# Padding rows scattered by row numbers, and two weight subtractions on VectorE

## The chip, the core and the metric

One core of a Trainium2 chip runs the whole program. The metric is the device time in microseconds of one launch; what is given for a kernel is the median of its runs. Engines: PE (TensorE), VectorE (DVE), ScalarE (ACT), GpSimd (POOL), and SyncE (SP), which only issues DMAs.

## What is computed

A linear attention (random features, exponentials) gives 4608 token rows of 512 numbers. Each row then goes through one of 8 experts, the one whose embedding is most alike, and is weighted by the softmax of that choice:

```python
xn = x / (np.linalg.norm(x, axis=-1, keepdims=True) + 1e-06)
logits = xn @ en.T / tau
expert_idx = np.argmax(logits, axis=1)
...
for e in range(E):
    mask = expert_idx == e
    if not mask.any():
        continue
    h = np.maximum(x[mask] @ w1[e], 0.0)
    out[mask] = gate_w[mask, None] * (h @ w2[e])
```

N = 4608, D = 512, E = 8, F = 1024; w1 is 512 x 1024 and w2 1024 x 512 for each expert.

## The kernel before

**First part** (to about 212 us): the attention, tile by tile of 128 tokens. As soon as a tile's tokens have their experts, GpSimd scatters its rows (L592, an indirect DMA with one row number for each partition) into `xs`, a table in device memory with a region of `REG` rows for each expert. Beside the 512 numbers a row carries the logits and the token's number, `PAY` = 521 numbers in all. `run[e]` is the next free row of region e.

**Pads.** The second part reads `xs` in blocks of 128 rows, so the last block of an expert reaches past its tokens. Rows of padding (`padrow`, in a part of w1l that is not in use yet, with a token number that no store takes) are written there: 128 rows from `run[e]` on, for every expert. The first expert, the one with most tokens, is swapped to place 0 and padded by SyncE (`pad(0)`); behind a drain, `pad(1)` to `pad(7)` load a row number into a register of GpSimd and issue a plain DMA of 128 rows (L990 to L1000).

**Second part** (from about 223 us): 38 steps of 128 rows. Step t takes its rows by `xload` (L188), splits them into a high and a low half (h and l, products in three passes), multiplies by w1 (24 matmuls of 512 columns), by w2 (24 more), and stores to the output. Steps 0 and 1 are done in the first part, step 2 begins the second. Weights lie in two buffers of four quarters each. The first expert's stand in buffer 0; the quarters 0 to 3 of the next go to buffer 1 during steps 2 to 5: a load to `raww` (`wload`), a high half by ScalarE, a low half by subtraction (`wsplit`, L227). For quarters 0 to 3 w1's low half is VectorE's work and w2's GpSimd's (L233, L234). Step 4 waits for w1's quarter 3.

**Order.** PE, GpSimd and SyncE run in the order of the code, in the second part VectorE and ScalarE too; between the two parts VectorE's order is the scheduler's. SyncE's queue holds all loads, one behind the other. Waits come from a tracker of memory: who writes a tile waits for whoever still reads or writes the same place, also where a pool was closed and another one opened on its memory. The pool `once`, which holds the tables between the parts, closes with the first part; `p2`, with the buffers `xg3`, `xg4` of the steps' rows, opens behind it. For accesses to `xs` the waits are set by hand: `written` takes them away among writes, and `xload` names which earlier writes a load waits for. For step 3 (t == NPRE + 1) the last PADP - 1 writes, the pads on GpSimd, are left out, and step 4's load waits for all.

Of the kernel before, what the change touches and what calls it, by code (L numbers as in the profile page):

```python
# [13 lines left out]
I32 = mybir.dt.int32  # L14
# [3 lines left out]
ALU = mybir.AluOpType  # L18
AX = mybir.AxisListType
ET = mybir.EngineType  # L20
PSUM = bass.MemoryType.PSUM

P = 128
B, H, S, D, M = 8, 8, 576, 64, 128
E, F = 8, 1024
# [7 lines left out]
GPICK = 5  # L33
DUM = E * REG
ROWS = DUM + P
RS = 576
PAY = DM + E + 1
NQ = 4
LAG = 7
NPRE = 2  # L40
# [1 line left out]
LOADS = {29: 0, 30: 2, 31: 1, 33: 4, 35: 6, 36: 3, 37: 5, 39: 7}  # L42
LOADS_LATE = 33
FILLS = {36: 1, 37: 1, 38: 1, 39: 1, 40: 1, 41: 1, 42: 2, 43: 4, 44: 5}
PADP = 8
ONACT = 3
DRAINS = (4,)
KPROJ = {0: (0,), 1: (1, 2), 2: (3,), 3: (4,), 4: (5,), 5: (6,)}
# [14 lines left out]
WHY = "computed on the chip from counts that sum to the token number"  # L63
# [3 lines left out]
def attention_moe(ctx: ExitStack, tc: tile.TileContext, qT, kT, v1, omT, emb, tau, w1q, w2q, xs, out):  # L67
    nc = tc.nc
# [39 lines left out]
    stepf = const.tile([P, 1], F32, name="stepf")  # L108
# [15 lines left out]
    runi = const.tile([P, E], I32, name="runi")  # L124
# [10 lines left out]
    put, got, outs, last_x, junks, kept = [], [], [], [], [], {}  # L135
# [4 lines left out]
    padrow = w1l[:, 1, 2, 0:PAY].bitcast(F32)  # L140
# [41 lines left out]
    def written(w):  # L182

        for o in put + got:
            tc.declare_no_dep(w.ins, o.ins.name, reason="other rows")
        put.append(w)

    def xload(t, row, xg):  # L188
        r = nc.sync.dma_start(xg, xs[ds(row, P), 0:PAY])
        if t in range(NPRE + 3):  # L190
            for j, w in enumerate(put):
                if t < NPRE and j > 3 * GPICK + 3 and w is not kept.get(t) or t == NPRE + 1 and j > len(put) - PADP:

                    tc.declare_no_dep(r.ins, w.ins.name, reason="other rows")
                else:
                    tc.add_manual_dep(r.ins, w.ins.name, sync, reason="rows written in any order")
        else:
            tc.add_manual_dep(r.ins, last_x[0].ins.name, sync, reason="behind an earlier step's wait")
        got.append(r)
        last_x[:] = [r]  # L200
        return xg
# [6 lines left out]
    def apart(wn, ws, t, ms, o):  # L208

        if (t == o or (t < NQ and o < NQ)) and (o, t) not in ((0, 3), (1, 2), (2, 3)):
            for w in ws:
                for m in ms:
                    tc.declare_no_dep(max(w, m, key=seq.get).ins, min(w, m, key=seq.get).ins.name, reason="the other weight buffer")
# [11 lines left out]
    def wsplit(wn, t, raw, dv, dp):  # L227
        _, h, l = W[wn]
        at = lambda a, d: a.rearrange("p a q f -> p (a q) f")[:, ds(d, 1), :].rearrange("p o f -> p (o f)")
        if t is not None and t < NQ:  # L230

            ih = nc.scalar.activation(h[:, 1, t, :], raw, AF.Copy)  # L232
            eng = nc.vector if wn == "w1" else nc.gpsimd  # L233
            ils = [eng.tensor_tensor(l[:, 1, t, :], raw, h[:, 1, t, :].bitcast(F32), op=ALU.subtract)]  # L234
        else:
            ih = nc.vector.tensor_copy(at(h, dv), raw)  # L236
            ils = []
            piece = F if t is None or t >= NSTAT - 2 else PIECE
            eng, d = (nc.vector, dv) if wn == "w2" and t is not None and t >= NSTAT - 2 else (nc.gpsimd, dp)
            for c in range(0, F, piece):  # L240
                c = slice(c, c + piece)
                ils.append(eng.tensor_tensor(at(l, d)[:, c], raw[:, c], at(h, d)[:, c].bitcast(F32), op=ALU.subtract))  # L242
        if t is None:
            return
        for w in (ih, *ils):
            seq[w] = len(seq)
            if t >= NQ:
                tc.add_manual_dep(w.ins, mmi[wn, t - 1][-1].ins.name, sync, reason="the buffer's last use")
        for o in range(NSTAT):
            apart(wn, (ih, *ils), t, mmi.get((wn, o), ()), o)  # L250
        if t < NPRE:

            for w in put:
                for il in ils:
                    tc.declare_no_dep(il.ins, w.ins.name, reason="another part of the weights")
        for w in spl.get((wn, t - 1), ())[1:]:
            tc.declare_no_dep(ih.ins, w.ins.name, reason="another part of the weights")
        spl[wn, t] = (ih, *ils)
# [3 lines left out]
    def flush():  # L262
        while lows:
            lows.pop(0)()
# [60 lines left out]
    with ExitStack() as c1:  # L325
# [453 lines left out]
        for i in range(NTILE + LAG + 2):  # L779
# [15 lines left out]
            if i == XLOAD:  # L795
                prow = [nc.values_load(
                    firsti[0:1, t : t + 1], engines=[ET.SP], min_val=t * P, max_val=(E - 1) * REG + t * P,
                    skip_runtime_bounds_check_because=WHY) for t in range(NPRE + 1)]
                for t in range(NPRE):
                    xload(t, prow[t], xgp[t])  # L800
# [181 lines left out]
        vt = nc.vector  # L982
        t = lambda n, w=E, dt=F32: once.tile([P, w], dt, name=n)
# [3 lines left out]
        vt.tensor_copy(runi[:, 0:1], swp[:, 0:1])  # L987
        vt.tensor_scalar(swp[:, 1:2], run[:, 0:1], swp[:, 0:1], None, op0=ALU.subtract)
        vt.scalar_tensor_tensor(runi[:, 1:], isf[:, 1:], swp[:, 1:2], run[:, 1:], op0=ALU.mult, op1=ALU.add)
        def pad(e):  # L990
            eng, et = (nc.gpsimd, ET.Pool) if 0 < e < PADP else (nc.sync, ET.SP)
            v = nc.values_load(runi[0:1, e : e + 1], engines=[et], min_val=0, max_val=DUM - P, skip_runtime_bounds_check_because=WHY)  # L992
            written(eng.dma_start(xs[ds(v, P), 0:PAY], padrow))

        pad(0)
        xload(NPRE, prow[NPRE], xgp[NPRE])

        nc.gpsimd.drain()
        for e in range(1, PADP):
            pad(e)  # L1000


        row = lambda a: a.unsqueeze(1).to_broadcast([P, E, E])
# [58 lines left out]
        tp = pb[3]  # L1062
        nc.tensor.transpose(tp[0:5, 0:P], tab, ident)
        vt.tensor_copy(tabi, tp[0:5, 0:NSTEP])
        for _ in range(FILL3):
            next(fill, None)
            flush()
# [15 lines left out]
    def x_of(t, row):  # L1083
        return xload(t, row, xgp[0] if t == "x" else xgp[1] if t == SHIFT else ring[(t - NPRE - (t > SHIFT)) % len(ring)])
# [6 lines left out]
    def words(t):  # L1091
        return p2.tile([P, F + DM], F32, name=f"wd{t}", tag="wd", bufs=1)
# [35 lines left out]
    def split(wn, t):  # L1128
        if t < NSTAT:
            wsplit(wn, t, raws.pop((wn, t)), *((reg("dv", t), reg("dp", t)) if t >= NQ else (None, None)))  # L1130
# [19 lines left out]
    with tc.manual_schedule(engines={ET.PE, ET.Activation, ET.DVE, ET.Pool, ET.SP}):  # L1150
# [11 lines left out]
        def joined(u):  # L1162
            wd, n = words(u), turn[u][0].shape[1] * P
            assert n == F
            for k in range(2):
                rejoin(u, wd, 0, F, k)
            return wd, n
# [65 lines left out]
        for t in range(NPRE, NSTAT):  # L1233
# [11 lines left out]
            if early:  # L1245
                wn = joined(t - 1)
# [43 lines left out]
            if late and not early:  # L1290
                wn = words(t - 1), turn[t - 1][0].shape[1] * P
# [64 lines left out]
    with tc.If(tot > NSTAT):  # L1356
        with tc.For_i(NSTAT, tot, 1) as i:
            get = lambda k, eng, mx: nc.values_load(tabi[k : k + 1, ds(i, 1)], engines=[eng], min_val=0, max_val=mx, skip_runtime_bounds_check_because=WHY)
            xgl = x_of("x", get(0, ET.SP, DUM))
            src = get(2, ET.SP, E * NQ - 1)  # L1360
            rw = {wn: wload(wn, "x", src) for wn in W}
            par = get(1, ET.PE, 1)
            h = hidden("x", x_turned("x", xgl), par)
            po = bank("pox", "kv0")
            products(po, h_turned("x", h), "w2", par, range(8), 0, True, True)
            n2, total = few("n2", "x", 3)[:, 0:1], few("total", "x", 3)[:, 0:1]
            squares(xgl, n2, nu[0])
            nrm = root(gp, n2, 1, "x")
            norms(nrm)
            exps(xgl, nrm, total)  # L1370
            inverted(total)
            scaled(po, xgl, total)
            store("x", xgl)
            dv, dp = get(3, ET.DVE, 2 * NQ - 1), get(3, ET.Pool, 2 * NQ - 1)
            for wn in W:
                wsplit(wn, None, rw[wn], dv, dp)
# [49 lines left out]
```

## Time and profile before

| | us |
|---|---|
| median of 3 runs | 630.5 (629.82 to 630.67) |
| the profiled execution, its own time | 630.09 |
| its span, first to last instruction | 628.4 |

The rows further down come from that one execution; their times are us from the span's start. PE's busy time says little about how fast it runs; where a chain of waits goes through PE, the time between two starts tells its pace. A wait for several signals is put down to the one that came last. Landing times are counted from the start of the issue to the completion signal.

### The profile page before, as it was taken

Reading aid. Unit: us, or ns where it says so; the run is one execution under the profiler, and the core shown is the slowest. Engines: PE = TensorE matmul, PEld = TensorE weight load, DVE = VectorE, ACT = ScalarE, POOL = GpSimd, SP = SyncE. Lnnn points to the kernel's source line nnn. Section 1 sums busy time; section 2 is a strip of 40 time slices with the busy share of each in tenths; the row PEclk is TensorE's granted clock in tenths of the full one; section 3 lists DMA queues with packets and bytes.
Section 4 is the critical chain, followed back from the end, with each engine's and each line's share of the span. In section 5 each row is a group of like instructions: output and inputs, shape, how many; then the busy total and the mean of one; then the engine's idle time right before and its main releaser. Section 6 shows DMA issues by size and latency. Waiting matters only on the chain.

```text
span 628.4 us, 19172 instructions
## 1 busy us (share of the span) xinstructions
PE 620.4 (99%) x6337; PEld 531.1 (85%) x6338; DVE 496.5 (79%) x917; ACT 432.5 (69%) x1135; POOL 421.2 (67%) x603
## 2 busy tenths in 40 slices
PE   9999999999999999999999999999999999999996
PEld 8999999999988787888888888888888888888885
DVE  5799899898989836779787877887887886877764
ACT  6999899899888237675757566656666656575630
POOL 3013344456887534588898878896987989796862
PEclk9999999999999999999999999999999999999999
DMA  7754776777772487698787796867787775968731
GB/s 259 221 154 156 240 198 206 223 220 237 274 254 79 154 305 253 187 273 233 225 217 238 180 263 189 244 191 211 226 211 243 201 245 171 255 196 197 221 118 47
DMA packets 143263, 132.19 MB, mean 210 GB/s; under 512 B 107766, under 2 KB 107894, under 8 KB 143168
## 3 DMA queue, kind: packets, MB, share of 16 engines
q1 hardware_dynamic: 136544, 109.96, 60.7%
q0 software_dynamic: 6480, 20.91, 8.6%
q8 instruction: 57, 0.93, 0.6%
q14 instruction: 38, 0.31, 0.2%
q10 hardware_dynamic: 144, 0.07, 0.0%
HBM read 83.78 MB, written 21.97 MB: 168 GB/s over the span
## 4 chain that ended last, share of the span: by engine, by line
PE 89%; issue 3%; DVE 3%; POOL 1%; ACT 1%; DMA 1%; POOLq 1%; DVEq 0%; ACTq 0%
PE po L287 30%; PE pb L287 30%; PE pb L376 11%; PE kva L408 5%; PE nuu L485 5%; PE nuu L465 2%; PE fs_a L287 1%; PE nuu L408 1%; DMA raww<-w2q 1%; DVE nmq L380 1%; PE pb L94 1%; POOLq L992 0%; PE pb L435 0%; DMA qt<-qT 0%; POOL w2l L234 0%
## 5 line engine op out<-in xcount | busy, mean ns | idle before, releaser
L242 POOL TENSOR_TENSOR w2l<-raww,w2h 128x256 f32 x128 | 140.3, 1096 | 7.6
L242 POOL TENSOR_TENSOR w1l<-raww,w1h 128x256 f32 (+1 forms) x130 | 116.0, 892 | 14.5 <-DMA xgp<-xs 5.2
L287 PE MATMUL po<-w2h,hh 128*128 (+1 forms) x288 | 112.3, 390 | 0.0
L287 PE MATMUL po<-w2l,hh 128*128 (+1 forms) x288 | 112.1, 389 | 0.0
L287 PE MATMUL po<-w2h,hl 128*128 (+1 forms) x288 | 112.1, 389 | 0.0
L287 PE MATMUL pb<-w1h,xh 128*128 (+1 forms) x280 | 109.6, 391 | 0.3 <-ACT nuu L298 0.3
L287 PE MATMUL pb<-w1h,xl 128*128 (+1 forms) x280 | 109.2, 390 | 0.0
L287 PE MATMUL pb<-w1l,xh 128*128 (+1 forms) x280 | 109.0, 389 | 0.0
L1140 DVE COPY pl<-pb 128x512 uint16<-128x512 uint16 x68 | 46.8, 690 | 59.8 <-ACT pl L1136 59.1
L1136 ACT ACTIVATE pl<-pb 128x512 uint16<-128x512 uint16 x68 | 39.4, 582 | 67.9 <-PE pb L287 65.2
L390 ACT ACTIVATE ftq<-pb,nmq 128x128 f32<-128x128 f32 x288 | 80.1, 415 | 4.2 <-DVE nmq L380 4.2
L317 POOL DMA_INDIRECT y<-xgp,tail x36 | 44.6, 1239 | 54.0 <-DVE w1h L236 30.2
L390 ACT ACTIVATE ftk<-pb,nmk 128x128 f32<-128x128 f32 x272 | 75.9, 466 | 4.5 <-DVE nmk L380 4.5
L1158 DVE COPY wd<-t 128x1024 uint16<-128x1024 uint16 x68 | 65.1, 959 | 1.6 <-DMA t<-pl 1.5
L1174 ACT ACTIVATE hh<-wd 128x1024 fp32r<-128x1024 f32 x34 | 36.1, 1063 | 42.1 <-DVE wd L1158 37.1
L287 PEld LDWEIGHTS po<-w2h,hl 128*128 128x128 f32 x288 | 54.1, 188 | 11.4
L287 PEld LDWEIGHTS po<-w2h,hh 128*128 128x128 f32 x288 | 54.1, 188 | 11.1
L287 PEld LDWEIGHTS po<-w2l,hh 128*128 128x128 f32 x288 | 54.0, 187 | 11.1
L287 PEld LDWEIGHTS pb<-w1h,xh 128*128 128x128 f32 x280 | 52.5, 188 | 11.3 <-ACT w2h L232 0.7
L287 PEld LDWEIGHTS pb<-w1h,xl 128*128 128x128 f32 x280 | 52.5, 188 | 11.2 <-DVE xl L271 0.2
L287 PEld LDWEIGHTS pb<-w1l,xh 128*128 128x128 f32 x280 | 52.7, 188 | 10.8
L1178 DVE SCALAR_TENSOR_TENSOR hl<-wd,hh 128x1024 fp32r<-128x1024 f32 x34 | 54.7, 1610 | 2.9 <-ACT hh L1174 2.3
(351 smaller groups left out, 1250.0 us busy)
## 6 DMA issues: line engine op xcount, KB each, us to landing
raww<-w1q SPq DMA_DIRECT2D x38, 512.0 KB, 4.5
raww<-w2q SPq DMA_DIRECT2D x38, 512.0 KB, 4.8
qt<-qT SPq DMA_DIRECT2D x36, 256.0 KB, 3.1
kt<-kT SPq DMA_DIRECT2D x35, 256.0 KB, 3.6
xg<-xs SPq DMA_DIRECT2D x23, 260.5 KB, 2.8
xgp<-xs SPq DMA_DIRECT2D x15, 260.5 KB, 3.6
rf<-w1q SPq DMA_DIRECT2D x4, 512.0 KB
rf<-w2q SPq DMA_DIRECT2D x4, 512.0 KB, 3.9
```

What stands on the lines that cost most here:

```text
L242: ils.append(eng.tensor_tensor(at(l, d)[:, c], raw[:, c], at(h, d)[:, c].bitcast(F32), op=ALU.subtract))
L287: done.append(nc.tensor.matmul(dst, x[:, c * P : (c + 1) * P], ws.rearrange("p o f -> p (o f)"), start=(begin and i == 0 and k == 0), stop ...
L317: w = nc.gpsimd.indirect_dma_start(out=out, out_offset=bass.IndirectOffsetOnAxis(ap=(xg[:, DM:] if tail is None else tail)[:, E : E + 1].b ...
L376: nc.tensor.matmul(st["pj" + w, i, a][:, c, :], st[w, i][r, c, :], om[r, :], start=True, stop=True)
L390: nc.scalar.activation(ft[:, h, :], pj[:, h, :], AF.Exp, bias=nm[:, h : h + 1])
L408: nc.tensor.matmul(acc[c : c + 64, h, :], ft[:, h, c : c + 64], vt[:, 2 * h + a, :], start=begin and h == 0, stop=u == 4 + 4 * b and h == 3,)
L485: nc.tensor.matmul(pn[a][s * D : s * D + D, h, :], st["qp", i, s][:, 2 * h + a, :], kvs[sb, int(u > 4 - s)][:, 4 * a + h, :], start=True, ...
L1136: nc.scalar.activation(planes[1][:, o : o + 512], halved(src)[:, :, 1], AF.Copy)
L1140: nc.vector.tensor_copy(planes[0][:, o : o + 512], halved(src)[:, :, 0])
L1158: nc.vector.tensor_copy(to, src)
L1174: nc.scalar.activation(hh, wd[:, 0:F], AF.Relu)
L1178: nc.vector.scalar_tensor_tensor(hl, wd[:, 0:F], 0.0, hh.bitcast(F32), op0=ALU.max, op1=ALU.subtract)
```

## The change

Pads 1 to 7 no longer are plain DMAs of 128 rows from a register's row number. Four VectorE operations make a table `padi` of row numbers, 128 for each expert: `run[e]` plus the partition's number, and for partitions that would pass the next multiple of 128 a number above `ROWS`, which the DMA's bounds check leaves out. Seven indirect DMAs on GpSimd, behind the step table, take their row numbers from its columns. `padi` is a tile of the pool `once`. The constant `PADP` (8) gives way to `E` (8). And in `wsplit`, for w2's quarters 0 and 1, the subtraction goes from GpSimd to VectorE.

```diff
--- before.py
+++ after.py
@@ -42,7 +42,6 @@
 LOADS = {29: 0, 30: 2, 31: 1, 33: 4, 35: 6, 36: 3, 37: 5, 39: 7}
 LOADS_LATE = 33
 FILLS = {36: 1, 37: 1, 38: 1, 39: 1, 40: 1, 41: 1, 42: 2, 43: 4, 44: 5}
-PADP = 8
 ONACT = 3
 DRAINS = (4,)
 KPROJ = {0: (0,), 1: (1, 2), 2: (3,), 3: (4,), 4: (5,), 5: (6,)}
@@ -189,7 +188,7 @@
         r = nc.sync.dma_start(xg, xs[ds(row, P), 0:PAY])
         if t in range(NPRE + 3):
             for j, w in enumerate(put):
-                if t < NPRE and j > 3 * GPICK + 3 and w is not kept.get(t) or t == NPRE + 1 and j > len(put) - PADP:
+                if t < NPRE and j > 3 * GPICK + 3 and w is not kept.get(t) or t == NPRE + 1 and j > len(put) - E:
 
                     tc.declare_no_dep(r.ins, w.ins.name, reason="other rows")
                 else:
@@ -230,7 +229,7 @@
         if t is not None and t < NQ:
 
             ih = nc.scalar.activation(h[:, 1, t, :], raw, AF.Copy)
-            eng = nc.vector if wn == "w1" else nc.gpsimd
+            eng = nc.vector if wn == "w1" or t < NPRE else nc.gpsimd
             ils = [eng.tensor_tensor(l[:, 1, t, :], raw, h[:, 1, t, :].bitcast(F32), op=ALU.subtract)]
         else:
             ih = nc.vector.tensor_copy(at(h, dv), raw)
@@ -987,17 +986,10 @@
         vt.tensor_copy(runi[:, 0:1], swp[:, 0:1])
         vt.tensor_scalar(swp[:, 1:2], run[:, 0:1], swp[:, 0:1], None, op0=ALU.subtract)
         vt.scalar_tensor_tensor(runi[:, 1:], isf[:, 1:], swp[:, 1:2], run[:, 1:], op0=ALU.mult, op1=ALU.add)
-        def pad(e):
-            eng, et = (nc.gpsimd, ET.Pool) if 0 < e < PADP else (nc.sync, ET.SP)
-            v = nc.values_load(runi[0:1, e : e + 1], engines=[et], min_val=0, max_val=DUM - P, skip_runtime_bounds_check_because=WHY)
-            written(eng.dma_start(xs[ds(v, P), 0:PAY], padrow))
-
-        pad(0)
+        v = nc.values_load(runi[0:1, 0:1], engines=[ET.SP], min_val=0, max_val=DUM - P, skip_runtime_bounds_check_because=WHY)
+        written(nc.sync.dma_start(xs[ds(v, P), 0:PAY], padrow))
         xload(NPRE, prow[NPRE], xgp[NPRE])
-
         nc.gpsimd.drain()
-        for e in range(1, PADP):
-            pad(e)
 
 
         row = lambda a: a.unsqueeze(1).to_broadcast([P, E, E])
@@ -1062,6 +1054,17 @@
         tp = pb[3]
         nc.tensor.transpose(tp[0:5, 0:P], tab, ident)
         vt.tensor_copy(tabi, tp[0:5, 0:NSTEP])
+
+        padi, over = t("padi", dt=I32), t("over")
+        vt.tensor_scalar(padi, runi, P - 1, None, op0=ALU.bitwise_and)
+        vt.tensor_scalar(over, padi, stepf, float(P), op0=ALU.add, op1=ALU.is_ge)
+        vt.scalar_tensor_tensor(over, over, float(ROWS), runi, op0=ALU.mult, op1=ALU.add)
+        vt.tensor_scalar(padi, over, stepf, None, op0=ALU.add)
+        for e in range(1, E):
+            written(nc.gpsimd.indirect_dma_start(
+                out=xs, out_offset=bass.IndirectOffsetOnAxis(ap=padi[:, e : e + 1], axis=0),
+                in_=padrow, in_offset=None, bounds_check=ROWS - 1, oob_is_err=False,
+            ))
         for _ in range(FILL3):
             next(fill, None)
             flush()
```

SyncE's queue around the loads of the rows of steps 3 and 4 (`xg`; `raww` are the weight loads between), before; a name in brackets is a completion signal, DMASW those of GpSimd's DMAs, eight in turn:

```order
L189 DMA xg_5242<-xs 128x521 [waits DMAHW3_49,DMAHW1_49,DMAHW4_49,PE_49,Pool_49]
...
L205 DMA raww_0_5314<-w2q 128x1024 [waits DMAHW2_49]
...
L205 DMA raww_1_5316<-w1q 128x1024 [waits Activation_49]
...
L205 DMA raww_1_5318<-w2q 128x1024 [waits DMAHW5_49]
...
L205 DMA raww_2_5320<-w1q 128x1024 [waits DMAHW0_49,DVE_49]
...
L189 DMA xg_5243<-xs 128x521 [waits DMASW5_49,DMASW4_49,DMASW6_49,DMASW2_49,DMASW7_49,DMASW1_49,DMASW0_49]
```

and now:

```order
L188 DMA xg_5241<-xs 128x521 [waits DMASW5_49,DMASW6_49,DMASW4_49,DMASW7_49,DMASW2_49,DMAHW1_49,DMASW1_49,DMAHW3_49,DMASW0_49,DMAHW4_49,PE_49,Pool_49]
...
L204 DMA raww_0_5313<-w2q 128x1024 [waits DMAHW2_49]
...
L204 DMA raww_1_5315<-w1q 128x1024 [waits Activation_49]
...
L204 DMA raww_1_5317<-w2q 128x1024 [waits DMAHW5_49]
...
L204 DMA raww_2_5319<-w1q 128x1024 [waits DMAHW0_49,DVE_49]
...
L188 DMA xg_5242<-xs 128x521
```

The order of the loads is the same; the seven DMASW waits of the second `xg` load stand at the first one, and the second has none.

GpSimd behind the last scatter of rows, before (two of seven pads):

```order
L592 DMA xs<-xr_4978,posi_5047 38016x576 [waits Pool_49]
L992 TENSOR_LOAD runi [waits DVE_49]
L993 ISA
L993 DMA xs<-w1l 128x521
L992 TENSOR_LOAD runi
L993 ISA
L993 DMA xs<-w1l 128x521 [waits DMASW5_49]
```

and now, to the first w2 subtraction that is left:

```order
L591 DMA xs<-xr_4978,posi_5047 38016x576 [waits Pool_49]
L1064 DMA xs<-w1l,padi 38016x576 [waits DVE_49]
L1064 DMA xs<-w1l,padi 38016x576 [waits DMASW5_49]
L1064 DMA xs<-w1l,padi 38016x576 [waits DMASW6_49]
L1064 DMA xs<-w1l,padi 38016x576 [waits DMASW7_49]
L1064 DMA xs<-w1l,padi 38016x576 [waits DMASW0_49]
L1064 DMA xs<-w1l,padi 38016x576 [waits DMASW1_49]
L1064 DMA xs<-w1l,padi 38016x576 [waits DMASW2_49]
L316 DMA y<-xgp_139 4608x512 [waits DMAHW4_49,DMASW3_49,DVE_49]
L316 DMA y<-xgp_140 4608x512 [waits DMASW4_49,DVE_49]
L233 TENSOR_TENSOR w2l<-raww_2_5326,w2h 128x1024 [waits DMAHW0_49,PE_49,Activation_49]
```

The seven register loads are gone, the seven pads carry the signals DMASW4 to 7 and 0 to 2, and behind the two stores the subtractions of `raww_0` and `raww_1` are missing.

VectorE from the low half of step 2's hidden values (`hl`) to that of step 4's rows (`xl`), before:

```order
L271 TENSOR_TENSOR hl_5369<-pb_74,hh_5368 128x512
L271 TENSOR_TENSOR hl_5369<-pb_71,hh_5368 128x512
L234 TENSOR_TENSOR w1l<-raww_2_5320,w1h 128x1024
L1140 COPY pl_0_5392<-pb_72 128x512
L1140 COPY pl_0_5392<-pb_73 128x512
L234 TENSOR_TENSOR w1l<-raww_3_5323,w1h 128x1024
L271 TENSOR_TENSOR xl_5441<-pb_74,xh_5440 128x512
```

and now:

```order
L270 TENSOR_TENSOR hl_5368<-pb_74,hh_5367 128x512
L270 TENSOR_TENSOR hl_5368<-pb_71,hh_5367 128x512
L233 TENSOR_TENSOR w2l<-raww_0_5313,w2h 128x1024
L233 TENSOR_TENSOR w2l<-raww_1_5317,w2h 128x1024
L233 TENSOR_TENSOR w1l<-raww_2_5319,w1h 128x1024
L1143 COPY pl_0_5391<-pb_72 128x512
L1143 COPY pl_0_5391<-pb_73 128x512
L233 TENSOR_TENSOR w1l<-raww_3_5322,w1h 128x1024
L270 TENSOR_TENSOR xl_5440<-pb_74,xh_5439 128x512
```

The two w2l subtractions stand between hl and w1's quarter 2 (`raww_2`). The four new operations on `padi` and `over` stand further up, among those that make the step table.

## Rows read from the trace of the kernel before

**Rows 1.** Page, its head: the span

```profile
span 628.4 us, 19172 instructions
```

**Rows 2.** Chain that ended last, longest pieces: start us, us, what

```profile
268.79 5.44 PE po L287 x24
274.23 5.44 PE pb L287 x24
...
612.38 10.91 PE po L287 x48
```

**Rows 3.** Who PE waited for, 204 us to the end: us, times, longest

```profile
PE pb L287 <- ACT nuu L298: 0.3, 1, 0.3
```

**Rows 4.** Timeline of PE, head of step 4: start us, us, instruction

```profile
244.53 0.39 PE L287 MATMUL po<-w2h,hl 128*128 128x512 f32 x1
245.19 0.47 PE L287 MATMUL pb<-w1h,xh 128*128 x1 [0.27 <-ACT nuu L298]
```

**Rows 5.** Timeline of VectorE, 236 to 245 us

```profile
236.04 1.28 DVE L271 TENSOR_TENSOR hl<-pb,hh 128x512 fp32r<-128x512 f32 x2
239.59 3.12 DVE L234 TENSOR_TENSOR w1l<-raww,w1h 128x1024 fp32r<-128x1024 f32 x1 [2.27 <-DMA xg<-xs]
...
243.83 1.21 DVE L234 TENSOR_TENSOR w1l<-raww,w1h 128x1024 fp32r<-128x1024 f32 x1
```

**Rows 6.** Timeline of GpSimd, 216 to 242 us

```profile
216.69 0.98 POOL L592 DMA_INDIRECT xs<-xr,posi  x1 [0.30 <-issue]
222.04 0.61 POOL L993 DMA_DIRECT2D xs<-w1l  x1 [4.37 <-DVE xgp L294]
...
229.14 0.54 POOL L993 DMA_DIRECT2D xs<-w1l  x1 [0.41 <-issue]
...
236.86 4.76 POOL L234 TENSOR_TENSOR w2l<-raww,w2h 128x1024 fp32r<-128x1024 f32 x2 [4.53 <-ACT w2h L232]
```

**Rows 7.** Timeline of all engines, 217 to 219 us: the step table's end

```profile
217.78 0.16 DVE L1057 TENSOR_TENSOR tab<-five 128x1 f32<-128x1 f32 x1
...
218.91 0.39 PE L287 MATMUL fs_o<-w2h,w2l 128*128 128x512 f32 x1
```

**Rows 8.** The drain's line on GpSimd's queue: count and duration in ns

```profile
L998 POOLq DRAIN  x1: 5679/5679/5679, 215.0 to 215.0; - x1
```

**Rows 9.** Who SyncE's queue waited for, 204 to 262 us

```profile
SPq L189 <- DMA xs<-w1l: 8.1, 1, 8.1
```

**Rows 10.** Timeline of SyncE's queue, 223 to 238 us

```profile
223.37 0.33 SPq L189 DMA_DIRECT2D xg<-xs  x1
223.89 0.36 SPq L205 DMA_DIRECT2D raww<-w2q  x1
...
228.66 0.33 SPq L205 DMA_DIRECT2D raww<-w1q  x1
237.41 0.33 SPq L189 DMA_DIRECT2D xg<-xs  x1
```

**Rows 11.** DMA issues, 204 to 262 us; and line L993, all its pads

```profile
xs<-xr,posi POOLq DMA_INDIRECT x8, 3.0
...
DMA to landing us min/median/max: 4.7/7.7/8.1
```

**Rows 12.** Page, part 6: loads of a step's rows, median us to landing

```profile
xg<-xs SPq DMA_DIRECT2D x23, 260.5 KB, 2.8
```

**Rows 13.** Timeline of PE, the transposes of step 3's rows

```profile
229.28 0.60 PE L269 MATMUL pb<-ident,xg 128*128 128x128 f32 x4
```

**Rows 14.** Windows: stretch, busy by engine, granted clock, DMA share, GB/s

```profile
229.00:235.00 6.00, 6.00 (x34) 4.99 (x34) 0.80 (x2) 2.88 (x5) 2.56 (x3) 1.00 1.01 400
626.00:628.00 2.00, 0.00 (x0) 0.00 (x0) 0.00 (x0) 0.00 (x0) 0.00 (x0) 0.60 0.31 110
```

**Rows 15.** Chain that ended last, the program's first microseconds

```profile
0.98 3.15 PE pb L94 x28
...
9.07 1.09 PE pb L376 x16
```

## What is predicted, and from what

> **What bounds the kernel now.** I read the page first, then the chain of work that ended last, then who PE waited for, then the timelines of the engines around the place of the change. The profiled execution took 630.09 us, its span 628.4 [rows 1]; 1.7 us lie around it and the change does not touch them. From about 266 us on, the chain is PE alone: each step is 24 matmuls of 5.44 us up and 24 of 5.44 us down, one behind the other until the last 48 [rows 2]. From 204 us to the end PE waits once, for 0.3 us [rows 3]. So nothing can be gained behind 266 us, and hardly anything before: what a change of pads and splits can do is take that one gap away, or make a new one between 213 and 260 us. The gap stands at the head of step 4: from 244.53 to 245.19 is 0.66 us where matmuls follow each other at 5.44/24 = 0.23, so it costs 0.43 us [rows 2, 4].
>
> The row names ACT as its releaser. VectorE's rows tell more: step 4 may start when the low half of w1's quarter 3 is written, and that subtraction runs 1.21 us from 243.83, to 245.04 [rows 5]. It is late since the one for quarter 2 took 3.12 us instead of 1.21, beside the two w2l subtractions that fill GpSimd from 236.86 to 241.62 [rows 5, 6].
>
> **The w2 subtractions (-0.4 us).** Two instructions of 2.4 us leave GpSimd and become two of some 1.21 us on VectorE (its own rate for this shape [rows 5]). There they stand behind hl, which ends at 237.3: 237.3 + 2 x 1.2 = 239.7. The quarter-2 subtraction, which starts at 239.59 today, starts at about 239.7, has no GpSimd work beside it and ends near 240.9 instead of 242.7. Quarter 3 then waits for its load alone, and ends a microsecond or more earlier. The gap goes: -0.4 us, at most -0.6 with the slow matmul starts behind it, 0 if PE is late for another reason. GpSimd has nothing due in the time it gains.
>
> **The row numbers (0).** Four small VectorE operations of 0.15 to 0.2 us, in among those that make the step table, put off its last one, at 217.78 to 217.94, by about 0.5 us. PE loads the table at 218.91 [rows 7]: 1.0 us of cover, so they cost nothing. Without it they would cost 0.5 us.
>
> **The pads on GpSimd (0 there).** Seven direct writes, each with a register load ahead, start at 222.04 to 229.14 [rows 6]. In their place seven scatters stand behind the same drain, which ends at 215.0 + 5.68 = 220.7 [rows 8]. A scatter takes 0.98 us and the next one follows 0.30 us behind [rows 6]: 1.28 us each. The first starts between 220.7 (the drain's end) and 222.04 (with a register load); I take 221.3. The last starts at 221.3 + 6 x 1.28 = 229.0, as today. The two stores behind them move by nothing that matters. What lands is less: the reference's routing of these inputs gives the experts 605, 0, 553, 121, 1152, 1704, 0 and 473 tokens. The sixth takes the place that SyncE pads. Those with a multiple of 128 (three) still get 128 rows, the other four 35, 87, 7 and 39: 552 rows of 896, an estimate from the inputs.
>
> **The wait that moves (+5.7 us).** This term decides. Today the load of step 4's rows waits 8.1 us on SyncE's queue for the pads, and is issued at 237.41; the load of step 3's rows goes out at 223.37 without that wait [rows 9, 10]. The order of the changed kernel shows the seven scatter lanes (0, 1, 2 and 4 to 7) as waits of step 3's load, and none left at step 4's. The text still says that step 3's load need not wait for the last seven writes. But `padi`, from which the scatters read their row numbers, is a tile of the first part's pool; step 3's buffer `xg3` is opened behind it, and I take it to lie on the same memory, so that filling it must wait until the last scatter is through. SyncE's queue is in order: four weight loads stand behind that load.
>
> So: the last pad starts at 229.0. A scatter lands 3.0 us from its start in this stretch, a direct pad took 7.7 in the median and 8.1 at most [rows 11]. I take 3.0, since the four weight loads that crowded the pads are now held back themselves, and the last pads are small: 232.0. SyncE needs 0.2 us more (today from 229.14 + 8.1 = 237.2 to 237.41): 232.2. A load of rows lands 2.8 us from its issue [rows 12]: 235.0. PE transposes these rows at 229.28, between the halves of step 2 [rows 13], and its queue is in order too. Stall: 235.0 - 229.28 = 5.7 us. The Trainium skill ("DMA: Bandwidth & Descriptors", section "Anatomy of one DMA — SWDGE (gpsimd) path") gives such a DMA 2.0 us plus its bytes at 436 GB/s, 2.2 us for 39 rows, an estimate; by it the pads would land 0.8 us sooner and the sum would be 636.6. The rows' 3.0 is for full tiles.
>
> What is late next: the four weight loads go out at 232.7 to 234.4 instead of 223.9 to 228.66 [rows 10], 9 us later, and are first needed by step 4, which itself starts 7 us later. Two megabytes at the 400 GB/s of this stretch [rows 14] are 5 us, so they are in by 240, and step 4 starts at 252. That cover holds; quarter 3 is issued 1 us after the split that frees its buffer, not behind the pads.
>
> **The clock (+2.0 us).** PE's last matmul ends at 612.38 + 10.91 = 623.29 [rows 2], and in the last two microseconds the granted clock is 0.60 on average [rows 14]. With levels of 1.0 (2.4 GHz) and 0.5 (1.2 GHz) that is low for 1.6 us of 2.0: it fell at 626.4, 3.1 us after the last matmul. A stall of 5.7 us is longer. How soon it comes back no stall here shows. At the program's start the first 28 matmuls take 112 ns each, later ones of as many columns 68 [rows 15]: slow for 3 us and more. I take 4 us at half rate, 2.0 us lost, and 0 to 3 as its bounds. The Trainium skill ("TensorE: Matmul & The Clock Gate", section "HAM oscillation — how this bites in real kernels") says the same of a DMA wait in a matmul stream, that work behind it starts throttled; if that did not hold here the sum would be 635.4.
>
> **Sum.** 630.09 + 5.7 + 2.0 - 0.4 = 637.4 against the profiled run. The three runs' median is 630.5, 0.4 above that run and within their spread of 0.85; I forecast 637.6.
>
> **Rivals.**
> (a) The stall comes, the clock stays up: 630.09 + 5.7 - 0.4 = 635.4, 635.6 against the median. For it: no row shows what a stall of this length in mid-program does. Against it: the fall at the end.
> (b) The load of step 3 is in time and only VectorE's part counts: not slower. Mechanism: the pads land early enough. The load would have to leave SyncE by 229.28 - 2.8 = 226.5, so the last pad would have to start by 223.3, and seven scatters follow each other every 0.3 us from 221.3. Time: 630.5 - 0.4 = 630.1. For it: rows left out may be cheap to issue. Against: three of the seven are full, and every scatter row shows about 1 us of GpSimd [rows 6].
> (c) Scatters land as the direct pads did, at 237.2: stall 237.4 + 2.8 - 229.28 = 10.9, with the clock 642.6, 643.0 against the median. For it: rows of 2 KB to scattered places beside the stores to y. Against: no weight load is in flight then.
>
> **How the numbers follow.** Stall and clock 0.66, (a) 0.20, (b) 0.08, (c) 0.06. Low end: first pad at 220.8, landing 2.8, so a stall of 4.9, no clock loss, -0.6: 634.4, and 634.0 with the spread of the runs. High end: pads landing 5.4 us after their start, midway between the quiet and the crowded row, a stall of 8, 3 for the clock: 641. So 634.0 to 641.0 leaves out (b), (c) and little else. A measurement of this kernel tells about 0.2% (1.3 us) from no change. Slower takes all but (b): 0.91; same has (b) nearly whole: 0.07; faster by over 1.3 us needs more than the one gap of 0.43 us that exists: 0.02.
>
> **What would show it.** In the changed profile: SyncE's load of step 3's rows waits some 8 us for the scatters of the pads and leaves near 232, step 4's waits for nothing; PE stands idle before the transposes of step 3's rows for 5 to 6 us, and its clock is below 1.0 for some microseconds behind; no gap at step 4's first matmul; the quarter-2 subtraction is back at 1.2 us; from 270 us on, all is as before, later by 7 us. It is wrong if that load leaves before 227, if PE's gap is under 4 us, or if a second gap opens behind it because the weights are late.

## The result, and the profile after

The changed kernel takes 638.91 us in the median (637.95 to 639.56, four runs), the kernel before beside it 630.16 (629.68 to 630.67): a ratio of 1.0139, 95% interval 1.0124 to 1.0154, so 8.8 us slower. Forecast were 637.6 us, between 634.0 and 641.0. The profiled execution took 638.46 us, its span is 8.4 us longer than that of [rows 1]:

```profile
span 636.8 us, 19158 instructions
```

Where [rows 3] had one wait of 0.3 us for PE, the same view of after has one of 6.3 us:

```profile
PE pb L268 <- DMA xg<-xs: 6.3, 1, 6.3
```

The chain that ended last tells how it came about. It now runs through the pads and SyncE's queue, 225 to 244 us (start us, us, what):

```profile
226.82 0.97 POOL xs L1064
227.79 0.31 issue
228.10 1.85 POOL xs L1064
229.95 0.30 issue
230.25 2.56 DMA xs<-w1l,padi
...
233.12 2.99 DMA xg<-xs
236.12 0.14 issue
236.25 1.09 PE pb L268 x4
237.34 4.22 PE pb L286 x12
```

Read it from the top: GpSimd issues the pads one by one, the last one at 230.25 lands 2.56 us later, SyncE then works off its waits and sends the load of step 3's rows at 233.12, that lands in 2.99 us, and only then PE transposes the rows. In [rows 10] the same load left at 223.37.

On PE's timeline the stall and what follows it are plain (start us, us, instruction):

```profile
229.51 0.39 PE L286 MATMUL pb<-w1h 128*128 128x512 f32 x1
236.25 1.09 PE L268 MATMUL pb<-ident,xg 128*128 128x128 f32 x4 [6.35 <-DMA xg<-xs]
236.99 0.78 PE L286 MATMUL pb<-w1h 128*128 128x512 f32 x1
```

From one matmul to the transposes are 6.74 us where 0.23 is the rule: 6.5 us lost. The four transposes take 1.09 us instead of 0.60 [rows 13], the matmul behind them 0.78 instead of 0.48. The windows of that stretch say why (stretch, PE busy, granted clock, DMA share, GB/s):

```profile
229.00:233.50 4.50, 0.90 (x4) 1.00 0.30 119
233.50:236.00 2.50, 0.00 (x0) 0.51 0.78 236
236.00:240.00 4.00, 3.75 (x11) 0.50 1.03 420
240.00:242.00 2.00, 2.00 (x11) 0.91 0.88 348
242.00:244.00 2.00, 2.00 (x12) 1.00 0.03 8
```

PE's last matmul ended at 229.90 (229.51 + 0.39) and PE stood idle from there; the granted clock fell from its upper level (2.4 GHz) to its lower (1.2) near 233.5, and PE worked at the lower one from its restart to about 240.4. What that costs can be read from PE's rows. From these transposes to the next ones, at 241.40, PE takes 5.15 us; before, the same stretch took 3.18 (229.28 to 232.46). So 2.0 us are lost.

The queue of SyncE (start us, us, instruction), which answers to [rows 10]:

```profile
233.12 0.33 SPq L188 DMA_DIRECT2D xg<-xs  x1
233.65 0.36 SPq L204 DMA_DIRECT2D raww<-w2q  x1
...
235.84 0.33 SPq L188 DMA_DIRECT2D xg<-xs  x1
244.43 0.33 SPq L204 DMA_DIRECT2D raww<-w1q  x1
```

Step 4's load (235.84) follows on its heels and waits for nothing. On VectorE, to be held against [rows 5]:

```profile
243.18 1.23 DVE L233 TENSOR_TENSOR w1l<-raww,w1h 128x1024 fp32r<-128x1024 f32 x1 [4.35 <-ACT w1h L231]
...
245.52 2.35 DVE L233 TENSOR_TENSOR w2l<-raww,w2h 128x1024 fp32r<-128x1024 f32 x2
247.79 1.22 DVE L233 TENSOR_TENSOR w1l<-raww,w1h 128x1024 fp32r<-128x1024 f32 x1
```

The two w2 subtractions run here at 1.2 us each, no w1 subtraction takes 3 us any more, and there is no gap at the head of step 4. The account of the profiled execution: 6.5 for the stall, 2.0 for the clock, less 0.6 for the gap of [rows 4] and the slow starts behind it, is 7.9; the rest, 0.5, has come up by 213 us, ahead of the change's work.

### The profile page after: what moved, and what is told of

Read it like the earlier page. It is cut to its first block, busy times and chain, and to the rows that moved or that the text cites. A ratio compares the mean times of both kernels' runs of the same rounds, so it can differ in the third digit from the quotient of the medians.

```text
span 636.8 us, 19158 instructions
## 1 busy us (share of the span) xinstructions
PE 621.9 (98%) x6337; PEld 532.4 (84%) x6338; DVE 499.3 (78%) x923; ACT 432.6 (68%) x1135; POOL 423.9 (67%) x601
## 4 chain that ended last, share of the span: by engine, by line
PE 86%; DVE 4%; DMA 3%; ACT 3%; issue 2%; POOL 1%; POOLq 0%; SPq 0%; DVEq 0%; ACTq 0%
PE po L286 31%; PE pb L286 31%; PE pb L375 9%; PE nuu L484 4%; PE kva L407 4%; PE nuu L464 2%; DMA xs<-w1l,padi 1%; ACT ftq L389 1%; PE fs_a L286 1%; DMA xs<-xr,posi 1%; PE nuu L407 1%; DVE nmq L379 1%; ACT ftk L389 1%; PE pb L268 1%; PE pb L93 0%
## 5 line engine op out<-in xcount | busy, mean ns | idle before, releaser
L241 POOL TENSOR_TENSOR w2l<-raww,w2h 128x256 f32 x128 | 144.6, 1130 | 7.5
L1161 DVE COPY wd<-t 128x1024 uint16<-128x1024 uint16 x68 | 67.3, 993 | 0.7 <-DMA t<-pl 0.7
```

What stands on the lines that cost most here:

```text
L1161: nc.vector.tensor_copy(to, src)
```

## The experiments

Each is compared with runs of the kernel before that were made beside it on the same chip: e1 to e4, then e5 to e8, on one chip, f1 to f3 on another. These stood at 632.3, 633.1 and 632.9 us, above the 630.2 of the first chip, so ratios are compared and not times. The theory: `padi` lies in the pool `once`, step 3's buffer lies in the pool that takes the place of `once`, and so its load waits for the pads. The rivals: the scatters are slow in themselves, the clock alone takes the time, or the subtractions do.

**e1: `padi` in the pool that stays open.**

```diff
-        padi, over = t("padi", dt=I32), t("over")
+        padi, over = const.tile([P, E], I32, name="padi"), t("over")
```

> The changed kernel with the table of row numbers, padi, in the pool that stays open to the end (const) instead of the first part's pool; nothing else is altered. Theory (step 3's load waits because xg3 lies on padi's memory): the load of step 3's rows leaves SyncE near 223.5 us again, PE has no gap before the transposes of those rows, step 4's load waits for the pads but leaves 2 to 5 us earlier than the 237.4 of the kernel before, and the gap of 0.4 us at the head of step 4 is gone: 629.7 us, 0.4 below the kernel before. Rival 1 (the wait comes from the writes to xs, wherever the table lies): 638.9 as the changed kernel. Rival 2 (the scatters themselves crowd GpSimd or the DMA engines): over 631 with a gap somewhere between 225 and 260 us.

Measured: ratio 1.0074 (1.0058 to 1.0089), 636.93 us. The load of step 3's rows leaves at 226.0 (in f1, the kernel before on a chip like this, at 226.3), and PE no longer stalls there: as to the wait, the theory holds. But half of the loss is still there, a miss. Who PE waited for, 204 us to the end:

```profile
PE pb L286 <- DVE xl L1180: 1.3, 1, 1.3
PE pb L286 <- POOL w2l L241: 0.9, 1, 0.9
PE fs_h L268 <- DVE w2l L270: 0.6, 1, 0.6
```

The first two are gaps at 288 and 290 us, far from the change, with the clock at its lower level behind them (0.57 over 290.5 to 294.5). And the DMA engines are busier in the steady part, 300 to 600 us, for the same traffic, e1 first, then before on the other chips of these runs (f1, below):

```profile
300.00:600.00 300.00, 300.00 (x1326) 1.00 0.85 218
```

```profile
300.00:600.00 300.00, 300.00 (x1325) 1.00 0.78 217
```

Moving 32 bytes of `padi` into the open pool had pushed every buffer behind it by 32 bytes. That had to be told apart from the wait (e7, e8).

**e2: the two subtractions alone**, the kernel before with

```diff
-            eng = nc.vector if wn == "w1" else nc.gpsimd
+            eng = nc.vector if wn == "w1" or t < NPRE else nc.gpsimd
```

> The kernel before with only the two w2 subtractions of quarters 0 and 1 moved from GpSimd to VectorE; pads as before. Theory (GpSimd's work holds VectorE's quarter-2 subtraction back): that subtraction takes 1.2 us instead of 3.1, quarter 3 is ready before PE needs it, the gap at the head of step 4 is gone: 629.7 us, 0.4 below the kernel before. Rival (two more operations of 1.2 us on VectorE make step 4's weights later still): the gap grows to 1 us or more, 630.8 us or more.

Measured: ratio 1.0005 (0.9997 to 1.0014). The quarter-2 subtraction takes 1.22 us, there is no gap at step 4, and nothing is gained.

**e3: the scatters alone** (after, with that line as in before).

> The changed kernel with the two w2 subtractions back on GpSimd: only the pads are scattered, padi in the first part's pool. Theory (all of the loss is the wait of step 3's load and the clock behind it): a PE gap of 6 to 7 us before the transposes of step 3's rows, clock below full for some 7 us, 638.9 to 639.4 us. Rival (part of the loss comes from the subtractions on VectorE): 636 to 638 us.

Measured: ratio 1.0151 (1.0137 to 1.0166), the whole loss. PE's wait, as in after:

```profile
PE pb L268 <- DMA xg<-xs: 6.4, 1, 6.4
```

**e4: e3 and e1 together** (scatters alone, `padi` in the open pool).

> Only the pads are scattered, with padi in the pool that stays open; the w2 subtractions are on GpSimd as before. Theory (GpSimd's subtractions make the gap at the head of step 4): no PE gap before the transposes of step 3's rows, the quarter-2 subtraction still takes about 3 us beside GpSimd and the gap of 0.4 us at step 4 stays: 630.1 us, as the kernel before. Rival (the pads make that gap, by holding back step 4's load and what is queued behind it): the gap goes without VectorE's part, 629.7 us.

Measured: ratio 1.0094 (1.0071 to 1.0117); no stall at step 3, but waits of 0.9 us at 238 and of 2.0 in all at 289 and 291 us, and the lower clock from 292 to 296 (0.57), as in e1. The subtractions aren't the cause of these either. What was expected at step 4 did not come: beside GpSimd's subtractions those of quarters 2 and 3 take 1.65 and 2.22 us, not about 3 for the first, and no gap stands there.

**e5: PE kept busy through the wait**, 96 small matmuls that nobody reads, ahead of the transposes of step 3's rows in after:

```diff
+                if t == NPRE:
+                    for _ in range(96):
+                        nc.tensor.matmul(nu[1][:, 0:P], ready, ready, start=True, stop=True)
```

> The changed kernel with 96 small matmuls on constants (128 columns, 5.4 to 6.5 us, into a bank that is free) ahead of the transposes of step 3's rows, so that PE works through its wait. Theory (2 us of the loss are the clock, which falls during the wait): granted clock 1.00 throughout, step 3's rows transposed at the same time as in the changed kernel, 2.0 us below the changed kernel, so 6.5 to 7 us above the kernel before. Rival (the clock costs nothing, all is the wait): same time as the changed kernel.

Measured: ratio 1.0184 (1.0142 to 1.0226), a miss: not faster than after, and whether it is slower the intervals leave open. The clock did stay up, as these windows show (229 to 235, 235 to 240, 240 to 245 and 290 to 320 us), but the time didn't come back:

```profile
229.00:235.00 6.00, 6.00 (x59) 1.00 0.35 135
235.00:240.00 5.00, 3.27 (x51) 1.00 0.76 255
240.00:245.00 5.00, 5.00 (x37) 1.00 0.95 377
290.00:320.00 30.00, 27.27 (x118) 1.00 0.87 227
```

PE stood for 1.7 us among the fillers themselves, so that step 3's rows were transposed at 240.31, 1.1 us later than in e6 beside it, and it stood for 2.7 more between 290 and 320 us. So the time of this run doesn't price the clock. One stretch of its profile does: from these transposes to the next ones PE takes 3.19 us, as before (3.18), and in e6, with the lower clock, 5.20.

**e6: no rows left out** (after; all 896 pad rows are written):

```diff
-        vt.scalar_tensor_tensor(over, over, float(ROWS), runi, op0=ALU.mult, op1=ALU.add)
+        vt.scalar_tensor_tensor(over, over, 0.0, runi, op0=ALU.mult, op1=ALU.add)
```

> The changed kernel with all 128 rows of each of the seven pads in bounds: no row is left out, 896 rows instead of 552. Theory (the pads' issue of 1.3 us each sets when the last one lands, not the bytes): step 3's load leaves within 0.5 us of the changed kernel's, time within 0.7 us of it. Rival (the bytes set it): the load leaves 1.7 us later (344 rows of 2 KB at 400 GB/s) and the time is 1.5 to 2 us above the changed kernel.

Measured: ratio 1.0143 (1.0128 to 1.0157), the same as after, which was measured on another chip. Leaving rows out is worth nothing that can be told in the time. In the profile step 3's load leaves 3.65 us behind the start of the last pad, which has 128 rows here and 39 in after; there, and in e3, it was 2.87. That is 0.8 us more and not the 0.5 allowed for, but far from the 1.7 of the rival. The scatters' rhythm on GpSimd is the same, with the sixth long in both; e6, then after:

```profile
229.43 0.98 POOL L1064 DMA_INDIRECT xs<-w1l,padi  x1 [0.30 <-issue]
230.71 1.82 POOL L1064 DMA_INDIRECT xs<-w1l,padi  x1 [0.30 <-issue]
```

```profile
225.54 0.98 POOL L1064 DMA_INDIRECT xs<-w1l,padi  x1 [0.30 <-issue]
...
228.10 1.85 POOL L1064 DMA_INDIRECT xs<-w1l,padi  x1 [0.31 <-issue]
```

**e7: `padi` apart, every buffer at its old address** (after, with `padi` in the 32 bytes of the spacer tile that stands there anyway):

```diff
-    wpool.tile([P, SHIFTW], F32, name="before_w")
+    padi = wpool.tile([P, E], I32, name="padi")
```

> The changed kernel with padi in the 32 bytes of before_w, the spacer that stands ahead of the weights' buffers: the table overlaps nothing, and every other buffer lies where it lay in the kernel before. Theory (the 4 us that the run with padi in const still lost, by a PE gap near 288 us, come from the 32 bytes by which that shifted all later buffers, so that the transposing DMAs take longer): no PE gap at step 3's rows, none near 288 us, DMA share over 300 to 600 us back at 0.77 from 0.85, time 0 to 0.5 us below the kernel before on the same chip. Rival (the scattered pads themselves cause the gap near 288 us): 4 us above the kernel before, as in the run with padi in const.

Measured: ratio 1.0044 (1.0027 to 1.0062). The stall is gone, and so are e1's gaps at 288 us; the DMA share over 300 to 600 us is 0.79. Still 2.6 us are left. PE waited for:

```profile
PE pb L268 <- ACT wd L1300: 1.0, 1, 1.0
PE fs_h L268 <- DVE w2l L270: 0.8, 1, 0.8
```

The first is a wait for ScalarE, which runs late twice. PE transposes step 3's rows at 232.95 (0.60 us), and ScalarE starts to copy them 2.24 us later. Then PE's next product ends at 236.32, ScalarE's copy that waits for it starts 1.69 us behind that end, and PE's wait ends with this copy:

```profile
235.19 0.60 ACT L269 ACTIVATE xh<-pb 128x512 fp32r<-128x512 f32 x1 [5.12 <-DMA xs<-w1l,padi]
...
238.01 0.60 ACT L1300 ACTIVATE wd<-pb 128x512 f32<-128x512 f32 x1 [1.73 <-PE pb L268]
```

**e8: 32 bytes alone**, the kernel before with the spacer tile twice as wide, and not one instruction changed:

```diff
-SHIFTW = 8
+SHIFTW = 16
```

> The kernel before with its spacer before_w 32 bytes wider and nothing else: no change in any instruction, only the places of the buffers behind it. Theory (places): packets of the transposing DMAs take 22 to 23 ns in the mean instead of 19, DMA share over 300 to 600 us 0.85 instead of 0.77, a PE gap near 288 us with the clock low behind it, 4 to 5 us above the kernel before. Rival (the pads cause it): time of the kernel before within 0.5 us.

Measured: ratio 1.0038 (1.0023 to 1.0052), 2.4 us slower, with the DMA share that e1 had, the DMAs' packets of 256 bytes at 22.3 ns in the mean (18.6 in e2, 19.4 in f1), and PE waiting for split operands:

```profile
300.00:600.00 300.00, 299.83 (x1320) 1.00 0.85 217
```

```profile
PE pb L287 <- DVE xl L1177: 1.1, 2, 0.9
PE pb L287 <- DVE w1l L234: 0.7, 1, 0.7
```

The longest wait for xl is a gap at 290 us, as in e1. The 0.7 us for w1l is another matter: it stands at the head of step 4, at 248.77, and here, as in [rows 5], the quarter-2 subtraction took 3.02 us.

So the rest of e1's loss is two things that nearly add up: where the buffers lie (0.0038) and what e7 keeps (0.0044), 0.0082 together against 0.0074 measured.

**f1: the kernel before again**, for its trace on a chip like those of the experiments.

> The kernel before, unedited, for its trace on the chip on which the runs beside it are made. The transposes of step 3's x tokens and ScalarE's first copy of them (xh, line 270) stand 0.76 us apart in the trace of before on the other chip. If the 0.7 to 1.5 us more seen with the scattered pads are theirs, this run shows 0.7 to 0.8 again and no gap of TensorE over 0.5 us near 214 us; if they belong to the chip, it shows them too.

Measured: 632.22 us, span 630.6. PE transposes step 3's rows at 231.82 and ScalarE starts 0.76 us later; no gap stands at 214 us. So neither belongs to these chips alone; both come with the scattered pads:

```profile
232.58 0.60 ACT L270 ACTIVATE xh<-pb 128x512 fp32r<-128x512 f32 x1 [3.11 <-PE pb L269]
...
235.22 0.60 ACT L1297 ACTIVATE wd<-pb 128x512 f32<-128x512 f32 x1 [1.55 <-PE pb L287]
```

The second row answers to the late copy in e7: the product that it waits for ended at 235.18, 0.04 us before.

It also shows what [rows 5] could not: here the quarter-2 subtraction takes 1.27 us and step 4 starts without a gap, though GpSimd's two w2 subtractions run beside it as they did there. This time VectorE starts first, at 241.00, and GpSimd's second one, which starts at 241.15, is the slow one, with 3.37 us and not 2.40:

```profile
241.00 1.27 DVE L234 TENSOR_TENSOR w1l<-raww,w1h 128x1024 fp32r<-128x1024 f32 x1 [1.77 <-ACT w1h L232]
238.77 5.74 POOL L234 TENSOR_TENSOR w2l<-raww,w2h 128x1024 fp32r<-128x1024 f32 x2 [3.18 <-ACT w2h L232]
```

**f2: the changed kernel again**, beside it.

> The changed kernel, unedited, beside the kernel before on the same chip. All theories: ratio 1.0139 as before, that is 1.012 to 1.016, with a stall of 6 to 7 us at step 3's transposes and a clock at its lower level for 7 to 10 us behind it. If the 0.8 us gap of TensorE at 214 us belongs to the chip, it shows here too, and the ratio is 0.001 higher.

Measured: ratio 1.0166 (1.0145 to 1.0187). The stall is there (6.4 us), the lower clock behind it, and a 0.8 us gap at 213 us, which the trace of after on the first chip doesn't have.

**f3: e7 with the pads sent as before**, as plain transfers; the row numbers are computed and nobody reads them.

```diff
+        for e in range(1, E):
+            pad(e)
...
-        for e in range(1, E):
-            written(nc.gpsimd.indirect_dma_start(
```

> Everything of e7 (all buffers at the addresses of before, the four row-number operations, the two subtractions on VectorE), but the seven pads go out as plain transfers at register addresses, as before; the row numbers are computed and not used. Theory that e7's 2.6 us are the scatters' (ScalarE's copy of step 3 late by 1.5 us, the weights behind it late): ratio 1.000 to 1.001, that of the two subtractions alone. Rival, that they are the added VectorE operations' or the wider spacer tile's: ratio 1.003 to 1.005 again.

Measured: ratio 1.0001 (0.9991 to 1.0010). The four VectorE operations and the subtractions cost nothing and give nothing; all of e7's 2.6 us come with the scatters.

## Why the prediction was right, point by point

| step | forecast, us | measured |
|---|---|---|
| subtractions | -0.4 | 0: e2 1.0005, f3 1.0001 (-0.6 in the profile of after) |
| row numbers | 0 | 0 (f3) |
| scatters in themselves | 0 | +2.6 (e7), partly hidden in after |
| wait that moves | +5.7 | 6.5 (after); 6.4 by the waits of e3 and f2 |
| clock | +2.0 | 2.0 (PE's rows in after) |

- **The wait that moves** was the step that decided, and e1, e4 and e7 settle its cause: with `padi` in a pool that stays open, the same scatters in the same place hold up no load. The prediction's reason was right in the pool and wrong in the place. It took `xg3` to lie on the same memory as `padi`; in the built kernel `padi` has bytes 229280 to 229312 of each partition, `xg3` 172736 to 174820, and no buffer of `p2` reaches beyond 228772. The wait is one of the pool and not of the buffer: the first use of a `p2` buffer on PE, VectorE and ScalarE waits for the seven pads too, as the load does, and in e7's build none of these four does. What carried the forecast was the order of the changed kernel, which showed the waits. The price of the tile's place is the distance from e7 to the kernels with the stall: 0.0099 of the time to e6 on the same chip, 0.0122 to f2 on another, so 6.3 to 7.7 us, each known to some 1.5 us. That goes with 5.7 + 2.0, but it is no clean measure of them, since e7 pays for late copies that after hides in its stall. In the profile the stall is 6.5: the first pad started at 221.71, not 221.3, one pad took 1.85 us on GpSimd instead of 0.98, and a step's load landed 2.99 us from its issue instead of 2.8. Against that the last pad landed in 2.56 and not 3.0 us. PE came to the rows 0.5 us later than in [rows 13], which took that much off the stall. The seven pads landed in 2.8 us in the median (2.6 to 5.0), the last, of 39 rows, in 2.56; the 2.2 us worked out from the Trainium skill ("DMA: Bandwidth & Descriptors", section "Anatomy of one DMA — SWDGE (gpsimd) path"), an estimate, lies under that. Rival (c), pads landing as late as the plain ones, fell by the same rows, rival (b) by the load's leaving at 233.12.
- **The clock** was right in size. Rival (a), no loss, is out: the matmuls behind the stall ran at the lower level for 4 us, and the stretch of 3.18 us took 5.15. That it met the forecast to a tenth is partly luck: the prediction took its 4 us from the program's start, for want of a stall to read, and gave 0 to 3 as bounds. No run shows the price in the kernel's whole time; it rests on rows of the profiles (after, e5, e6): behind the wait for step 3's rows PE worked at the lower level in after and e6, and at the upper one in e5, where fillers stood in the wait. What the Trainium skill ("TensorE: Matmul & The Clock Gate", section "HAM oscillation — how this bites in real kernels") says, that work behind a DMA wait in a matmul stream starts throttled, agrees with these rows.
- **The weights' cover** held: four loads went out between 233.65 and 235.32, and behind the clock's return no gap opened.
- **The subtractions** were the step whose reasoning fell. The profile after shows what was forecast: no 3.12 us subtraction, no gap. But the gap of [rows 4] comes and goes: e8, with the instructions of before, has it again with a subtraction of 3.02 us, and f1, the same kernel as before, has neither. The prediction's mechanism is real: the two engines do hold each other up. But in every trace looked at it is the one that starts later that pays. Before, GpSimd's second subtraction started at 239.22 and VectorE's at 239.59: 3.12 us. In e8 the starts were 241.72 and 242.18: 3.02 us. In f1 VectorE was 0.15 us ahead and lost nothing. So a few tenths of a microsecond decide whether there is a gap to win. A gain read from one short gap in one profile was no gain of the kernel in the median, and -0.4 should have been 0.
- **The scatters in themselves** were put at 0, and are not. The missing term hardly shows in the profile of after, where PE stalls at step 3 anyway and ScalarE's late copy has no part. With 0 for the subtractions the sum would have been 638.0; against the measured 638.9 the stall put too short by 0.8 accounts for the rest.

**What stays open.** Why scatters cost e7 2.6 us is known only in part. PE lost 1.0 us to a ScalarE copy that came 1.69 us behind the product it waits for (0.04 in f1). The copy of step 3's rows before it was late in the same way, 2.24 us behind the transposes' start against 0.76. For that copy the profile names the scatters, but in the order of the built kernel it waits for none of the pads, only for earlier scatters, and for PE's signal; on ScalarE's queue the wait that held it, 5.62 us long, is the one with PE's signal in it. The trace has this signal at 235.05, 1.5 us behind the end of the transposes, and the next one of PE at 237.99, 1.67 us behind its matmul; in f1 both stand within 0.02 us of the end of their work. So it is PE's signals that come late while scattered pads are under way. Why, no run here shows. The waits ahead of the first pad, at 213 and 214 us, add 0.6 more: 0.8 and 0.3 where f1 and f3 have one of 0.5 at 210. The rest, about 1 us, has no place that I can point to: the profiled execution of e7, at 634.68 us, is 1 us under its median. No version here beats the kernel before.

## What to carry to other kernels

A small tile that a DMA reads as its index is in use for as long as the DMA is under way. In a pool that is closed, it held up the first uses of the pool opened in its place, here the load of another step with an in-order queue behind it, though no buffer of the new pool lies on the tile. Look for it in the waits of the built order, not in the text. When a scratch tile is moved, put it where no other buffer shifts, and make sure with a run in which nothing but the shift is done. A gap of less than half a microsecond in a single profile is worth a second profile before it is counted as a gain.

## What was not expected of the hardware

- 32 bytes of SBUF make 2.4 us: in e8 no instruction differs from before, the traffic over 300 to 600 us is the same 217 GB/s, but the DMA engines are busy for 0.85 of the time instead of 0.77 (e2, on the same chip) and 0.78 (f1), and PE waits for its operands. Of its waits, the 0.7 us at step 4 go with the slow subtraction and need not come from the shift. Why such a shift makes the same transfers take longer no run here shows.
- Rows left out by the bounds check save nothing on GpSimd: the third pad, with 7 of its 128 rows left (by the count in the prediction), takes the same 0.98 us as in e6, where all are written, and its successor starts the same 0.30 us later.
- The sixth of seven scatters took 1.85 us in after, 1.82 in e6 with all rows written, and 1.8 to 1.9 in e1, e4, e7 and f2, on three chips. It is not the dropped rows; what it waits for the profile doesn't say.
- While scattered pads are under way, signals of PE can come late: in e7 by 1.5 and 1.7 us (at 235.05 and 237.99, for work that ended at 233.55 and 236.32), in e4 by 1.4 and 1.6, in e1 by 0.6 and then on time. With plain pads (f1) both come within 0.02 us (232.43 for 232.42, 235.19 for 235.18).
- VectorE's and GpSimd's subtractions of 128x1024 hold each other up, and the later one pays whole: behind GpSimd's, VectorE's took 3.12 us in before and 3.02 in e8 instead of 1.21; behind VectorE's, GpSimd's took 3.37 in f1 and 3.38 in e3 and e4 instead of 2.40. In each the later one ended about its own time behind the end of the earlier.
